# A spectral mixer with a GEGLU FFN: FFN weight groups 3 and 4 loaded early into the buffer of the last down weights, nine half-blocks instead of eight, and one operand read from PSUM

## The chip, the cores and the metric

The kernel runs on one core of one Trainium2 chip. The metric is the device time of one execution in microseconds (us). A core has five engines that run side by side, each with its own instruction queue: TensorE (PE in the profile, with its weight loads as PEld), VectorE (DVE), ScalarE (ACT), GpSimd (POOL) and SyncE (SP). In this kernel SP only issues DMA transfers, in the order of its queue.

## The reference, cut to what matters

```python
def _A_ref(x, w_r, w_i):                       # x: 1 x 2048 x 576, bf16
    X = jnp.fft.rfft2(x.astype(jnp.float32), axes=(-2, -1))
    X = X * (w_r + 1j * w_i)
    return jnp.fft.irfft2(X, s=(S, D), axes=(-2, -1)).astype(jnp.bfloat16)

def _B_ref(x, w_gate, w_up, w_down):           # w_gate, w_up: 576 x 4608; w_down: 4608 x 576
    return (_gelu(x @ w_gate) * (x @ w_up)) @ w_down

h  = x + _A_ref(_layernorm(x), A_w_r, A_w_i)
h2 = h + _B_ref(_layernorm(h), B_w_gate, B_w_up, B_w_down)   # the output
```

## The kernel before, in words

Everything stays on the chip in bf16 and is written out by hand: the program fixes the order of the instructions on each engine (a manual schedule), and the tile pools only decide which buffer a tile gets, so what an instruction waits for is its data, its buffer, and its turn on its engine.

**Spectral part (up to about 68 us).** The 2048 rows are 16 slabs `h` of 128. The two-dimensional FFT is done as products with sine and cosine tables on TensorE. For each of eight pairs of row frequencies (`order` = 1, 2, ..., 7, 0, called channels here) these steps run, staggered over the iterations `i` of one loop:

- `f2` (L478) makes two column transforms in PSUM; `f2_out` (L489) copies each to SBUF as `pq`, on ScalarE.
- `f3(k, 0)` and `f3(k, 1)` (L495, L496) make the row step, each into one PSUM tile `gh_ps`; L514 copies them on ScalarE to SBUF as `g` and `hs`.
- `sums_of(k)` (L523, L524) makes `g - hs` and `g + hs` on VectorE into `xab`.
- `wmul` (L543, L548, L549, L562, L530) multiplies `xab` with the filter on VectorE and leaves the result in `Zt`. The last of these operations for one channel, L530, is held back until the next channel's products are done.
- `i3` (L592) loads `Zt` as weights and transforms back, two iterations after `f3`.
- `inv_cols` (L643) and `add_rows` (L766) finish the inverse transform and `h_sb` becomes `h`.

All PSUM tiles of the kernel share one pool of four tiles (`two`): an engine that still reads one holds up the later matmul that gets its place.

**FFN (from about 68 us).** The 16 slabs go in four chunks of 512 rows. In each chunk the 36 feature blocks `f` of 128 go through `gate` (L894): 18 matmuls give gate and up products in one PSUM tile, ScalarE applies the GELU (L902) and VectorE multiplies (L903) into `P_sb`. Three blocks are one weight group, loaded by `load_gu` (L144) as two DMAs, gate and up, of 432 KB each, in a pool of three buffers. When the three blocks of a group are issued, the group is popped and the group three further on is loaded into its buffer. After the 36 blocks of a chunk the down product runs (L937), with the down weights `w_down` in three buffers of 12 blocks each: `wd_a`, `wd_0` and `wd_1` (the trace calls the last two `wd`).

The start of chunk 0 is special. Its slabs 2 and 3 are not ready when TensorE is, so the first `NH` = 8 blocks are done as **half-blocks**: first on the 256 columns of slabs 0 and 1, later, when blocks 0 to 7 come round in the main loop, on the other 256 columns. In between, slabs 2 and 3 are normalised (`norm2`, L791) and turned by a transposing DMA (`flip`, L803) into `Bt`. The list `after` names what is put between the first half-blocks; the dictionary `todo` puts the remaining work of the spectral part (`fold`, `add_both`, `stats2`, `norm2`, `flip`) and the pieces of the third down-weight buffer (`load_wd2`, L738) behind certain blocks of the main loop.

SP's queue around the change, in order: weight groups 0 to 2 (L144, from 37.69 us on), `wd_a` (L695), the second down-weight buffer (`load_wd(1)`, L728, issued at 59.35 us, when the last reader of the memory that it takes over is done), the flips of slabs 2 and 3 (L803), then group 3 when group 0 is popped, group 4, and so on.

Of the kernel before, what the change touches and what calls it, by code (L numbers as in the profile page):

```python
# [12 lines left out]
BF16 = mybir.dt.bfloat16  # L13
# [7 lines left out]
P = 128  # L21
S = 2048
H = 16
D = 576
# [6 lines left out]
NR = D // 64  # L31
# [3 lines left out]
FQ = 3  # L35
# [6 lines left out]
def kernel_body(  # L42
# [11 lines left out]
    nc = tc.nc  # L54
# [7 lines left out]
    wgpool = ctx.enter_context(tc.tile_pool(name="wgu", bufs=3))  # L62
# [3 lines left out]
    def two(name):  # L66
        return psum.tile([P, 2, 512], FP32, name=name, tag="two", bufs=4)
# [69 lines left out]
            dst, h_sb[:, h, :], m[:, h, 0:1], r[:, h : h + 1], op0=ALU.subtract, op1=ALU.mult  # L137
        )

    def load_gu(g):  # L140
        gc = slice(g % (NFT // FQ) * FQ * P, (g % (NFT // FQ) + 1) * FQ * P)
        t = wgpool.tile([P, NR, FQ * P], BF16, name="wgu", tag="wgu")
        for c, w in ((0, B_w_gate), (1, B_w_up)):
            nc.sync.dma_start(t[64 * c : 64 * c + 64, :, :], w[:, gc].rearrange("(r k) c -> k r c", k=64))  # L144
        return t

    spec = tc.tile_pool(name="spec", bufs=1)
# [8 lines left out]
    wd_view = B_w_down.rearrange("(ft p) d -> p ft d", p=P)  # L156
    NWA = 12
    wd_a = keep.tile([P, NWA, D], BF16, name="wd_a")
# [303 lines left out]
    gk, hk = {}, {}  # L462
    zt = {}
    order = [1, 2, 3, 4, 5, 6, 7, 0]
# [29 lines left out]
    def comb(dst, k1, t0, a, t1, b):  # L494
        T.matmul(dst, lhsT=TF[:, ts[k1], t0, :], rhs=a, start=True, stop=False)  # L495
        T.matmul(dst, lhsT=TF[:, ts[k1], t1, :], rhs=b, start=False, stop=True)  # L496

    def f3(k, half):
        ps = two("gh_ps")
        if k == 0:  # L500
            p0, p8 = pq[0], pq[8]
            t0, t1 = (NS, C) if half else (C, SN)
            for b, kk, p in ((0, 0, p0), (1, 8, p8)):
                comb(ps[:, b, 0:J], kk, t0, p[:, 0, 0:J], t1, p[:, 1, 0:J])
            if half == 0:
                xab[k] = wk.tile([P, 2, 2, JP], BF16, name="xab", tag="xab", bufs=2)
            A.copy(xab[k][:, half, :, 0:J], ps[:, :, 0:J])
            return
        p, q = pq[k], pq[k + 8]
        gh = wk.tile([P, 2, JP], BF16, name="hs" if half else "g", tag="hs" if half else "g", bufs=2)  # L510
        r = half
        comb(ps[:, r, 0:J], k, C, p[:, r, 0:J], SN, q[:, r, 0:J])
        comb(ps[:, 1 - r, 0:J], k, C, q[:, r, 0:J], NS, p[:, r, 0:J])
        A.copy(gh[:, :, 0:J], ps[:, :, 0:J])  # L514
        if half == 0:
            gk[k] = gh
            return
        hk[k] = gh
# [151 lines left out]
    n = len(order)  # L670
    for i in range(n + 1):
# [12 lines left out]
        if 1 <= i <= n:  # L684
            f3(order[i - 1], 0)
            f3(order[i - 1], 1)
            if i == 1:
                f2_out(order[1])
                sums_of(order[0])
            else:  # L690
                if i == 2:
                    cosine(rest)
                    turn_tf(rest)
                    pre = [load_gu(g) for g in range(3)]
                    nc.sync.dma_start(wd_a[:], wd_view[:, 0:NWA, :])  # L695
                wmul(order[i - 2], i - 1, order[i - 1])
# [24 lines left out]
    fp = ctx.enter_context(tc.tile_pool(name="ffn", bufs=1))  # L721
    NP0 = 22
    P_sb = [fp.tile([P, NP0, 4 * P], BF16, name="P_sb")]
    cwb = fp.tile([P, 5, 2, JP], FP32, name="cwb", tag="P1")[:]
    wd = [wd_a] + [fp.tile([P, NWA, D], BF16, name=f"wd_{i}") for i in range(2)]

    def load_wd(i):
        nc.sync.dma_start(wd[i][:], wd_view[:, i * NWA : (i + 1) * NWA, :])  # L728

    def p_sb(f):  # L730
        if f >= NP0 and len(P_sb) == 1:
            P_sb.append(fp.tile([P, NFT - NP0, 4 * P], BF16, name="P_sb", tag="P1"))
        return P_sb[f // NP0][:, f % NP0, :]

    load_wd(1)

    def load_wd2(s):
        nc.sync.dma_start(wd[2][:, s], wd_view[:, 2 * NWA : 3 * NWA][:, s])  # L738


    ln2 = {}
    both = {}
# [128 lines left out]
    todo = {}  # L871
# [8 lines left out]
        todo.setdefault(b + 1, []).append((flip, h))  # L880

    for i in range(0, NWA, 2):
        todo.setdefault(10 + 3 * i // 2, []).append((load_wd2, slice(i, i + 2)))
    blk = 0
    groups = pre
    NG = NFT // FQ

    def gate(tcnk, f, w, i, lo, hi):
        n = hi - lo
        gu = two("gu")  # L890
        for r in range(NR):
            for c in range(2):
                rows = slice(64 * c, 64 * c + 64)
                T.matmul(  # L894
                    gu[:, c, 0:n],
                    lhsT=w[rows, r, i * P : (i + 1) * P],
                    rhs=hl[tcnk % 2][rows, r, lo:hi],
                    start=(r == 0),
                    stop=(r == NR - 1),
                )  # L900
        g_sb = roll.tile([P, D], FP32, name="g_sb", tag="g_sb", bufs=3)[:, 0:n]
        A.activation(g_sb, gu[:, 0, 0:n], ACT.Gelu_apprx_tanh)  # L902
        V.tensor_tensor(p_sb(f)[:, lo:hi], g_sb, gu[:, 1, 0:n], ALU.mult)  # L903

    NH = 8
    after = {
        0: [(sum_squares, 3), (norm2, 2), (flip, 2)],
        1: [(head_rstd, 3)],
        2: [(norm2, 3), (flip, 3)],
    }  # L910
    for f in range(NH):
        gate(0, f, groups[f // FQ], f % FQ, 0, 2 * P)
# [4 lines left out]
    for tcnk in range(4):  # L917
        for gi in range(NG):
            for i in range(FQ):
                f = gi * FQ + i  # L920
                gate(tcnk, f, groups[0], i, 2 * P if tcnk == 0 and f < NH else 0, 4 * P)
                for fn, h in todo.pop(blk, ()):
                    fn(h)
                blk += 1
            groups.pop(0)
            n = tcnk * NG + gi + 3
            if n < 4 * NG:
                groups.append(load_gu(n))
        for st in range(4):
            h = tcnk * 4 + st  # L930
            if h < H - 1:
                accs = [two("acc") for _ in range(2)]
                for f in range(NFT):
                    for c in range(2):
                        for i in range(2):
                            rows = slice(64 * i, 64 * i + 64)
                            T.matmul(  # L937
                                accs[i][:, c, 0:DH],
                                lhsT=p_sb(f)[rows, st * P : (st + 1) * P],
                                rhs=wd[f // NWA][rows, f % NWA, c * DH : (c + 1) * DH],  # L940
                                start=(f == 0),
                                stop=(f == NFT - 1),
                            )
                part = roll.tile([P, D], FP32, name="part", tag="g_sb", bufs=3)[:].rearrange("p (b n) -> p b n", b=2)
                A.copy(part, accs[0][:, :, 0:DH])  # L945
                V.tensor_tensor(part, part, accs[1][:, :, 0:DH], ALU.add)  # L946
                hv = h_sb[:, h, :].rearrange("p (b n) -> p b n", b=2)
                V.tensor_tensor(hv, hv, part, ALU.add)  # L948
                if tcnk == 3:
                    nc.sync.dma_start(out_view[:, h, :], h_sb[:, h, :])  # L950
                continue
            for c in range(2):
                cc = slice(c * DH, (c + 1) * DH)
                acc = two("acc")
                for f in range(NFT):
                    T.matmul(  # L956
                        acc[:, 0, 0:DH],
                        lhsT=p_sb(f)[:, st * P : (st + 1) * P],
                        rhs=wd[f // NWA][:, f % NWA, cc],
                        start=(f == 0),  # L960
                        stop=(f == NFT - 1),
                    )
                V.tensor_tensor(h_sb[:, h, cc], h_sb[:, h, cc], acc[:, 0, 0:DH], ALU.add)
                nc.sync.dma_start(out_view[:, h, cc], h_sb[:, h, cc])
        if tcnk < 3:
            nc.sync.dma_start(
                out_view[:, tcnk * 4 : (tcnk + 1) * 4, :],
                h_sb[:, tcnk * 4 : (tcnk + 1) * 4, :],
            )


@with_exitstack
def kernel(
    ctx: ExitStack,
    tc: tile.TileContext,
    A_x: bass.AP,
    A_w_r: bass.AP,
    A_w_i: bass.AP,
    B_x: bass.AP,
    B_w_gate: bass.AP,  # L980
    B_w_up: bass.AP,
    B_w_down: bass.AP,
    out: bass.AP,
):
    kernel_body(tc, A_x, A_w_r, A_w_i, B_x, B_w_gate, B_w_up, B_w_down, out)
# [30 lines left out]
```

## Time and profile before

| | |
|---|---|
| time, median of 3 runs | 500.18 us (499.68 to 500.25) |
| the profiled execution, its own time | 499.93 us |
| its span in the trace | 498.1 us |
| granted TensorE clock over the span | 0.999 of full speed |
| busy in the span | PE 489.0, PEld 320.1, DVE 223.2, ACT 162.0, POOL 29.3 us |
| DMA traffic | 62.33 MB |

The span is the time between the first and the last recorded work; the 1.8 us beside it belong to the start and the end of the execution. Busy time of an engine is the sum of its instructions' times, with overlaps counted once. Matmuls are pipelined: one has a recorded time of several times the distance to the next one, so a wait looks shorter in the idle column than what it costs.

In a row of the timeline the columns are: start (us), length (us), engine, line, operation, output <- input, shape, xcount, and in brackets the idle time of the engine before it with what ended it. SPq rows are DMA issues in SP's queue. A row of the windows gives, for a stretch of time, the busy time and number of instructions of each engine, then the granted clock, the busy share of the DMA engines, and GB/s.

### The profile page before, as it was taken

The numbers are of one execution on the slowest core, as the hardware profiler recorded it, in microseconds if no ns is written. First come the engines' busy times: TensorE is split into PE (matmuls) and PEld (weight loads), VectorE is DVE, ScalarE is ACT, GpSimd is POOL, SyncE is SP. The second block draws the span as 40 slices with busy tenths as digits, with TensorE's granted clock in tenths as the row PEclk, the third lists the DMA queues.
The fourth block names the chain that finished last, engine by engine and source line by source line (L and its number), as shares of the span: only waits on it lengthen the run. The fifth ranks groups of instructions, "written<-read, shape, count | busy, mean of one in ns | idle before, by whom it ended". The sixth has DMA issues, their size and how long they took to land.

```text
span 498.1 us, 12611 instructions
## 1 busy us (share of the span) xinstructions
PE 489.0 (98%) x5642; PEld 320.1 (64%) x5644; DVE 223.2 (45%) x442; ACT 162.0 (33%) x287; POOL 29.3 (6%) x78
## 2 busy tenths in 40 slices
PE   7999999999999999999999999999999999999997
PEld 3567788444479964444499944444799644445995
DVE  8989786788641234433311245333211333333111
ACT  8989983232210013223200132332110223233000
POOL 8500010101100000000000000000000000000000
PEclk9999999999999999999999999999999999999999
DMA  8729845999990019998830079987700288880000
GB/s 280 222 60 194 217 140 102 204 208 213 192 193 15 2 50 185 205 176 154 158 76 3 3 159 191 193 160 153 145 3 3 71 157 158 158 150 2 14 13 25
DMA packets 89549, 62.33 MB, mean 125 GB/s; under 512 B 23190, under 2 KB 88086, under 8 KB 89494
## 3 DMA queue, kind: packets, MB, share of 16 engines
q1 hardware_dynamic: 89206, 60.34, 61.3%
q0 software_dynamic: 288, 1.18, 0.8%
q8 instruction: 44, 0.72, 0.6%
q14 instruction: 11, 0.09, 0.1%
HBM read 52.65 MB, written 2.36 MB: 110 GB/s over the span
## 4 chain that ended last, share of the span: by engine, by line
PE 90%; DMA 2%; ACT 0%; SPq 0%; issue 0%; DVE 0%
PE gu L894 54%; PE acc L937 27%; PE cs_ps L643 2%; PE acc L956 2%; PE eo_ps L592 2%; DMA wgu<-in_B_w_up_dram 1%; PE pq_ps L478 1%; PE y_ps L766 1%; DMA Bt<-hrow 1%; PE gh_ps L496 0%; PE gh_ps L495 0%; PE eo_ps L616 0%; PE pt L835 0%; ACT hs L514 0%; SPq L144 0%; ACT pq L489 0%
## 5 line engine op out<-in xcount | busy, mean ns | idle before, releaser
L894 PE MATMUL gu<-Bt,wgu 64*128 64x512 bf16 (+1 forms) x2736 | 284.5, 365 | 0.7 <-DMA wgu<-in_B_w_up_dram 0.5
L894 PEld LDWEIGHTS <-wgu 64*128 64x128 bf16 x2736 | 135.0, 94 | 146.1 <-DMA wgu<-in_B_w_up_dram 1.4
L903 DVE TENSOR_TENSOR P_sb<-g_sb,gu 128x512 bf16<-128x512 f32 (+1 forms) x152 | 99.6, 657 | 144.7 <-ACT g_sb L902 144.7
L902 ACT ACTIVATE g_sb<-gu 128x512 f32<-128x512 f32 (+1 forms) x152 | 87.3, 575 | 195.0 <-PE gu L894 194.7
L937 PEld LDWEIGHTS <-P_sb 64*128 64x128 bf16 x2160 | 132.7, 94 | 0.6
L937 PE MATMUL acc<-wd,P_sb 64*128 64x288 bf16 x1440 | 93.8, 283 | 0.0
L946 DVE TENSOR_TENSOR part<-part,acc 128x576 f32<-128x576 f32 x15 | 11.3, 754 | 111.3 <-ACT part L945 111.3
L937 PE MATMUL acc<-wd_a,P_sb 64*128 64x288 bf16 x720 | 49.7, 283 | 0.0
L945 ACT COPY part<-acc 128x576 f32<-128x576 f32 x15 | 9.6, 639 | 122.4 <-PE acc L937 122.4
L285 PE MATMUL f2t<-h_sb,ident 128*128 128x512 bf16 x26 | 9.1, 510 | 3.6 <-DMA h_sb<-in_A_x_dram 3.6
L478 PE MATMUL pq_ps<-DT,Bt 128*128 128x290 bf16 x64 | 12.2, 286 | 0.2 <-DVE Bt L327 0.2
L791 DVE TENSOR_SCALAR hrow<-h_sb,mv,rstd 128x1152 bf16<-128x1152 bf16 x14 | 12.1, 867 | 0.6 <-POOL rstd L829 0.6
L948 DVE TENSOR_TENSOR h_sb<-h_sb,part 128x576 bf16<-128x576 bf16 x15 | 11.4, 758 | 0.5
L133 POOL TENSOR_TENSOR rstd<-rstd,mhalf 128x1 f32<-128x1 f32 (+1 forms) x16 | 11.2, 701 | 1.3
L643 PE MATMUL cs_ps<-DQ,EO 58*128 58x290 bf16 x144 | 11.0, 283 | 0.0
L478 PEld LDWEIGHTS <-Bt 128*128 128x128 bf16 x96 | 9.3, 97 | 2.6
L132 POOL TENSOR_SCALAR rstd<-mv 128x1 f32<-128x1 f32 (+1 forms) x16 | 3.9, 246 | 101.1 <-DVE mv L118 100.8
L297 PE MATMUL f2t<-F,xn 128*128 128x256 bf16 x64 | 9.2, 275 | 0.6 <-DVE xn L136 0.6
L489 ACT CAST pq<-pq_ps 128x580 bf16<-128x580 f32 x15 | 9.6, 668 | 0.0
L123 ACT ACTIVATE junk<-h_sb 128x576 bf16<-128x576 bf16 x14 | 9.4, 676 | 0.4 <-DMA h_sb<-in_A_x_dram 0.4
L643 PEld LDWEIGHTS <-EO 58*128 58x128 bf16 x160 | 8.3, 94 | 2.0 <-issue 0.4
L117 DVE BATCH_NORM_STATS2 st<-h_sb 128x6 f32<-128x288 bf16 x21 | 9.3, 442 | 0.0
(135 smaller groups left out, 265.7 us busy)
## 6 DMA issues: line engine op xcount, KB each, us to landing
wgu<-in_B_w_gate_dram SPq DMA_DIRECT2D x48, 432.0 KB
wgu<-in_B_w_up_dram SPq DMA_DIRECT2D x48, 432.0 KB
wd_a<-in_B_w_down_dram SPq DMA_DIRECT2D x1, 1728.0 KB
wd<-in_B_w_down_dram SPq DMA_DIRECT2D x1, 1728.0 KB
wd<-in_B_w_down_dram SPq DMA_DIRECT2D x6, 288.0 KB
out_dram<-h_sb SPq DMA_DIRECT2D x3, 576.0 KB
h_sb<-in_A_x_dram SPq DMA_DIRECT2D x4, 288.0 KB
h_sb<-in_A_x_dram SPq DMA_DIRECT2D x2, 576.0 KB
```

What stands on the lines that cost most here:

```text
L133: G.tensor_tensor(dst[:, sl], dst[:, sl], mhalf[:, sl], ALU.pow)
L478: T.matmul(ps[:, par, 0:JP], lhsT=Bt[:, t, col], rhs=DT[:, t // 2, par] if t < 4 else DF[:, par], start=(t == par), stop=(t == 4),)
L592: T.matmul(pv[:, n], lhsT=z[:, a, w].rearrange("p b j -> p (b j)"), rhs=TI[:, ts[k], 1 - a : 3 - a, :], start=(a == 0), stop=(a == 1),)
L643: T.matmul(ps[:, e, 0:JP], lhsT=EO[x][rows, w, 2 * g : 2 * g + 2].rearrange("p h e k l -> p (h e k l)"), rhs=DQ[rows, w] if w or e else DT ...
L791: V.tensor_scalar(hrow[:], h_sb[:, h, :].rearrange("p (r k) -> p r k", k=64).unsqueeze(2).to_broadcast([P, NR, 2, 64]), mv2[:, h, 0:1], rs ...
L894: T.matmul(gu[:, c, 0:n], lhsT=w[rows, r, i * P : (i + 1) * P], rhs=hl[tcnk % 2][rows, r, lo:hi], start=(r == 0), stop=(r == NR - 1),)
L902: A.activation(g_sb, gu[:, 0, 0:n], ACT.Gelu_apprx_tanh)
L903: V.tensor_tensor(p_sb(f)[:, lo:hi], g_sb, gu[:, 1, 0:n], ALU.mult)
L937: T.matmul(accs[i][:, c, 0:DH], lhsT=p_sb(f)[rows, st * P : (st + 1) * P], rhs=wd[f // NWA][rows, f % NWA, c * DH : (c + 1) * DH], start=( ...
L946: V.tensor_tensor(part, part, accs[1][:, :, 0:DH], ALU.add)
L948: V.tensor_tensor(hv, hv, part, ALU.add)
L956: T.matmul(acc[:, 0, 0:DH], lhsT=p_sb(f)[:, st * P : (st + 1) * P], rhs=wd[f // NWA][:, f % NWA, cc], start=(f == 0), stop=(f == NFT - 1),)
```

## The change

It has three parts.

1. The buffer of the third 12 down-weight blocks (tag `wd_2`) is first used as a tile `early` of two weight groups, which has the same size. `load_wd(1)` goes from its place before the FFN to the list `after`, behind the flip of slab 3; in its old place groups 3 and 4 are loaded into `early` (four DMAs). Popping groups 0, 1 and 2 now loads groups 5, 6 and 7; popping 3 and 4 loads nothing; from group 5 on each pop loads the group three further on. The pieces of the third down-weight buffer, which can only come when group 4 has been used, go from behind blocks 10, 13, ..., 25 to behind blocks 16, 19, ..., 31.
2. `NH` is 9 instead of 8: block 8 is also done as two half-blocks.
3. For the first channel (`order[0]` = 1), `f3(1, 1)` leaves its result in PSUM: the ScalarE copy to `hs` is left out, and `sums_of(1)` reads the second operand of both VectorE operations from the PSUM tile (fp32) instead of SBUF (bf16).

```diff
-    def load_gu(g):
+    def load_gu(g, t=None):
         gc = slice(g % (NFT // FQ) * FQ * P, (g % (NFT // FQ) + 1) * FQ * P)
-        t = wgpool.tile([P, NR, FQ * P], BF16, name="wgu", tag="wgu")
+        if t is None:
+            t = wgpool.tile([P, NR, FQ * P], BF16, name="wgu", tag="wgu")[:]
...
         comb(ps[:, 1 - r, 0:J], k, C, q[:, r, 0:J], NS, p[:, r, 0:J])
+        if k == order[0] and half:
+            hk[k] = ps
+            return
         A.copy(gh[:, :, 0:J], ps[:, :, 0:J])
...
-    wd = [wd_a] + [fp.tile([P, NWA, D], BF16, name=f"wd_{i}") for i in range(2)]
+    wd = [wd_a, fp.tile([P, NWA, D], BF16, name="wd_1")]
...
+    def load_wd2(s):
+        if len(wd) == 2:
+            wd.append(fp.tile([P, NWA, D], BF16, name="wd_2", tag="wd_2"))
+        nc.sync.dma_start(wd[2][:, s], wd_view[:, 2 * NWA : 3 * NWA][:, s])
...
-    load_wd(1)
...
+    early = fp.tile([P, 2, NR, FQ * P], BF16, name="wgu_e", tag="wd_2")
+    pre += [load_gu(3 + i, early[:, i]) for i in range(2)]
...
     for i in range(0, NWA, 2):
-        todo.setdefault(10 + 3 * i // 2, []).append((load_wd2, slice(i, i + 2)))
+        todo.setdefault(16 + 3 * i // 2, []).append((load_wd2, slice(i, i + 2)))
...
-    NH = 8
+    NH = 9
     after = {
         0: [(sum_squares, 3), (norm2, 2), (flip, 2)],
         1: [(head_rstd, 3)],
-        2: [(norm2, 3), (flip, 3)],
+        2: [(norm2, 3), (flip, 3), (load_wd, 1)],
     }
...
             groups.pop(0)
-            n = tcnk * NG + gi + 3
-            if n < 4 * NG:
-                groups.append(load_gu(n))
+            n = tcnk * NG + gi
+            if n not in (3, 4):
+                n += 5 if n < 3 else 3
+                if n < 4 * NG:
+                    groups.append(load_gu(n))
```

More of the change, by code (lines that the diff above doesn't have):

```diff
@@ L138, in normalise @@
         )
-    def load_gu(g):
+    def load_gu(g, t=None):
         gc = slice(g % (NFT // FQ) * FQ * P, (g % (NFT // FQ) + 1) * FQ * P)
-        t = wgpool.tile([P, NR, FQ * P], BF16, name="wgu", tag="wgu")
+        if t is None:
+            t = wgpool.tile([P, NR, FQ * P], BF16, name="wgu", tag="wgu")[:]
         for c, w in ((0, B_w_gate), (1, B_w_up)):
-            nc.sync.dma_start(t[64 * c : 64 * c + 64, :, :], w[:, gc].rearrange("(r k) c -> k r c", k=64))
+            nc.sync.dma_start(t[64 * c : 64 * c + 64], w[:, gc].rearrange("(r k) c -> k r c", k=64))
         return t
@@ L733, in p_sb @@
         return P_sb[f // NP0][:, f % NP0, :]
-    load_wd(1)
-    def load_wd2(s):
-        nc.sync.dma_start(wd[2][:, s], wd_view[:, 2 * NWA : 3 * NWA][:, s])
+    early = fp.tile([P, 2, NR, FQ * P], BF16, name="wgu_e", tag="wd_2")
+    pre += [load_gu(3 + i, early[:, i]) for i in range(2)]
     ln2 = {}
```

## The prediction

> **What bounds the kernel now.** I read the page first, then the waits of TensorE, then the chain that ended last in order of time.
>
> ```profile
> span 498.1 us, 12611 instructions
> ...
> PE 489.0 (98%) x5642; PEld 320.1 (64%) x5644; DVE 223.2 (45%) x442; ACT 162.0 (33%) x287; POOL 29.3 (6%) x78
> ```
> ```profile
> PE gh_ps L496 <- ACT pq L489: 0.5, 2, 0.3
> PE gu L894 <- DMA wgu<-in_B_w_up_dram: 0.5, 1, 0.5
> PE gh_ps L495 <- ACT TF L255: 0.2, 1, 0.2
> PE gu L894 <- DMA Bt<-hrow: 0.2, 1, 0.2
> ```
>
> TensorE sets the time: it is busy for 489.0 of 498.1 us. The change removes no TensorE work, so it can only win back waits. The waits list (total us, times, longest) names three that it aims at: `pq` in the spectral part, the up half of a weight group, and the flip. In the chain, behind 68 us, all is TensorE but for these two transfers, start and length in us:
>
> ```profile
> 74.19 3.45 DMA Bt<-hrow
> ```
> ```profile
> 81.60 7.25 DMA wgu<-in_B_w_up_dram
> ```
>
> The flip of slab 3 lands at 74.19 + 3.45 = 77.64, weight group 3 at 81.60 + 7.25 = 88.85.
>
> **What the two FFN waits really cost.** Idle time understates a wait, since a matmul's recorded time runs past the start of the next. I take the loss from the follower: ScalarE's GELU starts once per block.
>
> ```profile
> 77.58 0.38 ACT L902 ACTIVATE g_sb<-gu 128x256 f32<-128x256 f32 x1 [0.60 <-PE gu L894]
> 78.97 0.39 ACT L902 ACTIVATE g_sb<-gu 128x256 f32<-128x256 f32 x1 [1.00 <-PE gu L894]
> ...
> 85.35 0.38 ACT L902 ACTIVATE g_sb<-gu 128x256 f32<-128x256 f32 x1 [0.60 <-PE gu L894]
> 86.33 0.38 ACT L902 ACTIVATE g_sb<-gu 128x256 f32<-128x256 f32 x1 [0.60 <-PE gu L894]
> 88.28 0.60 ACT L902 ACTIVATE g_sb<-gu 128x512 f32<-128x512 f32 x1 [1.56 <-PE gu L894]
> 91.05 0.60 ACT L902 ACTIVATE g_sb<-gu 128x512 f32<-128x512 f32 x1 [2.17 <-PE gu L894]
> ```
>
> An undisturbed half-block takes 86.33 - 85.35 = 0.98 us, an undisturbed full block (block 8) 88.28 - 86.33 = 1.95. Between block 7's first half (77.58) and block 0's second half (78.97) lie 1.39: **0.41 lost** to the flip. Between block 8 (88.28) and block 9 (91.05) lie 2.77: **0.82 lost** to group 3.
>
> **Part 1, groups 3 and 4 early.** What moves is SP's queue.
>
> ```profile
> 59.35 0.37 SPq L728 DMA_DIRECT2D wd<-in_B_w_down_dram  x1
> 72.00 4.28 SPq L803 DMA_TRANSPOSE Bt<-hrow  x2
> 80.93 0.63 SPq L144 DMA_DIRECT2D wgu<-in_B_w_gate_dram  x1
> ```
> ```profile
> 41.50:52.00 10.50, 10.50 (x91) 8.39 (x88) 10.50 (x25) 10.22 (x19) 0.00 (x0) 1.00 1.13 200
> ```
> ```profile
> 78.00:80.00 2.00, 2.00 (x42) 2.00 (x38) 0.84 (x2) 0.43 (x2) 0.00 (x0) 1.00 0.00 0
> 80.00:82.00 2.00, 2.00 (x42) 2.00 (x38) 1.63 (x5) 0.80 (x3) 0.00 (x0) 1.00 0.00 0
> ```
>
> The four new DMAs take the place of the issue at 59.35, behind the same waits, and 4 x 0.63 = 2.5 us of SP's time. Their 4 x 432 KB = 1.77 MB go at the rate of weight groups, 200 GB/s (the window in which groups 0 to 2 arrive), in 8.8 us: landed by about 70, where block 9 needs them at about 87.7. The 0.82 goes whole. They end some 2 us before the flips at 72.00.
>
> `load_wd(1)` is moved past both flips, which end their issue at 76.28. SP has nothing due from there until group 0 is popped, about 81.5, and the DMA engines stand idle (0 GB/s from 78 to 82), so its issue of 0.37 us delays nobody. Its 1.77 MB, at 200 GB/s if it is no faster than a weight group, are in by about 86.5. They are first read in the down product:
>
> ```profile
> 143.96 35.25 PE acc L937 x574
> ```
>
> What is late next? Group 5 is issued at 81.5 and needed by block 15, at 87.7 + 6 x 1.95 = 99.4 at the earliest; with the rest of `wd_1` ahead of it, its 0.88 MB are in by 91. Groups 6 and 7 have as much time. The pieces of the third down buffer come six blocks later; the last, behind block 31, goes out at about 133 (143.96 less the 1.2 won and five blocks), and its first reader, block 34 of the down product, comes 34 x 4 matmuls of 35.25/574 us behind the chunk's end, at about 151. I take 0 for all of it.
>
> **Part 2, the ninth half-block.**
>
> ```profile
> 77.77 5.09 PE L894 MATMUL gu<-Bt,wgu 64*128 64x256 bf16 x90 [0.23 <-DMA Bt<-hrow]
> ```
> ```profile
> 88.97 1.01 DVE L903 TENSOR_TENSOR P_sb<-g_sb,gu 128x256 bf16<-128x256 f32 x2
> ```
>
> Without the wait the second halves would begin at 77.77 - 0.41 = 77.36; with one more half-block in front, at 78.34. The flip lands at 77.64, 0.7 us earlier: the 0.41 goes. The price is two half-blocks for one full block, 2 x 0.98 - 1.95 = **+0.01**, and one more GELU and product on engines that wait for TensorE. What could be late next is VectorE, which is behind there: its products of blocks 7 and 8 end at 88.97 + 1.01 = 89.98; moved by 0.57 with the second halves, about 90.5. The next matmuls to take their PSUM tiles are those behind block 10, at about 87.7 + 3.9 = 91.6. 1.1 us are left; beyond that each us counts whole.
>
> **Part 3, the sum out of PSUM.**
>
> ```profile
> 28.23 0.64 ACT L514 CAST g<-gh_ps 128x578 bf16<-128x578 f32 x1 [0.74 <-PE gh_ps L496]
> 28.76 0.65 ACT L514 CAST hs<-gh_ps 128x578 bf16<-128x578 f32 x1
> ```
> ```profile
> 29.44 0.47 DVE L523 TENSOR_TENSOR xab<-g,hs 128x578 bf16<-128x578 bf16 x1 [0.79 <-ACT hs L514]
> 29.82 0.46 DVE L524 TENSOR_TENSOR xab<-g,hs 128x578 bf16<-128x578 bf16 x1
> 30.37 0.77 DVE L543 TENSOR_TENSOR m<-xab,WR 128x1156 bf16<-128x1156 bf16 x1
> ```
> ```profile
> 83.65 1.41 DVE L777 TENSOR_TENSOR h_sb<-h_sb,y_ps 128x576 bf16<-128x576 bf16 x2
> ```
> ```profile
> 61.22 0.82 DVE L663 TENSOR_SCALAR cs<-cs_ps 128x580 bf16<-128x580 f32 x1 [1.50 <-PE cs_ps L643]
> ```
>
> L523 now waits for `hs`, which ends at 29.41. After the change it waits for `g`, which ends at 28.87, so it starts at about 28.90, 0.54 earlier. But its second operand is then fp32 in PSUM. The nearest row is L777, the same operation on a bf16 and a PSUM operand of 576: two in 1.41. From 28.90 the pair ends at 30.31. L543 starts 0.09 behind the end of L524 (29.82 + 0.46 = 30.28) now, so 30.40 then: **+0.03**. Bounds: the pair could keep today's 0.84, giving -0.54; by L663, the slowest VectorE read of PSUM that I found, 2 x 0.82 give +0.26. I take the row with the same operation.
>
> [...]
>
> Does the 0.03 reach the end?
>
> ```profile
> 30.40:35.60 5.20, 4.57 (x33) 3.00 (x32) 5.10 (x11) 5.01 (x9) 0.00 (x0) 1.00 0.15 32
> ```
> ```profile
> 35.12 0.45 DVE L530 TENSOR_TENSOR Zt<-zb,za 128x580 bf16<-128x580 bf16 x1
> ```
> ```profile
> 35.64 1.00 PEld L592 LDWEIGHTS <-Zt 128*128 128x128 bf16 x10 [0.36 <-issue]
> ```
> ```profile
> 30.55 0.28 PE L496 MATMUL gh_ps<-pq,TF 128*128 128x289 bf16 x1 [0.26 <-ACT pq L489]
> ```
>
> VectorE is busy for 5.10 of the 5.20 us behind L543, up to L530, which ends at 35.57; `i3` loads that `Zt` as weights and starts at 35.64, after a gap. So this chain passes its shift on. Dropping a ScalarE copy of 0.65 also lets `pq` come earlier, and the wait at 30.55 (and its like in the next channel) shrinks; but TensorE then meets the same 35.64. I take 0 for that, and +0.03 for the part.
>
> **Sum:** -0.82 - 0.41 + 0.01 + 0.03 = **-1.19 us**, on the profiled execution 499.93 -> 498.74. That execution is 0.25 under the median of the runs, 500.18, which I take as the base: 500.18 - 1.19 = **499.0**. I call 0.2% (1.0 us) the bound, about what a measurement of this kernel can tell from no change; the forecast lies just beyond it.
>
> **Rivals.**
>
> *A wait stays (inside the bound).* `wd_1` goes out right behind flip 3 (76.28), which lands only at 77.64; if it shares the DMA engines with the flip, the flip may lose its 0.7 to spare and more, up to the 0.41 again. Or part 3 costs L663's 0.26. Then -1.19 + 0.41 = -0.78, or -1.19 + 0.23 = -0.96: about 499.3. For it: L663 exists. Against it: group 3, issued at 80.93, moved nothing before 82, so a new DMA comes late for that; and L777 is the closer operation.
>
> *ScalarE is the releaser (more gain).* The chain in order of time has this in front of `i3`:
>
> ```profile
> 34.97 0.66 ACT hs L514
> ```
>
> It ends at 35.63. If ScalarE's queue sets that start, one copy less moves it by the 0.4 that TensorE loses at 30.55 (0.26 idle and its overlap): -1.6, 498.6. Against it: `Zt` comes from L530 at 35.57, and VectorE's chain in front has no hole, so at best 0.06 should come of it.
>
> *Early groups block the flips (slower).* The place is the DMA engines at 72.00. Group 3 itself took from 80.93 to 88.85, 7.9 us for 0.88 MB, 112 GB/s. At that rate groups 3 and 4 would land at 59.35 + 15.8 = 75.2; the flips queued behind would land 3.2 late, at 80.8, and the second halves start there, 2.5 after the forecast's 78.34: -1.19 + 2.5 = +1.3, 501.5. It decides from a landing after 72.7 on (below 133 GB/s). Against it: 200 GB/s held over 10.5 us with groups back to back, and those 7.9 us hold the start-up and the first part of group 4.
>
> **Chances and range.** Forecast 0.62, a wait stays 0.22, ScalarE 0.08, flips blocked 0.06, others, half of them slower, 0.02. Since the runs of before spread over 0.57, a sixth of the forecast's share falls within the bound. Faster by over 0.2%: 0.52 + 0.08 = 0.60; within: 0.10 + 0.22 = 0.32; slower by over 0.2%: 0.08, rounded up. The range for 8 in 10 goes from the ScalarE case less half the spread, 498.3, to a kept wait and the dear end of part 3 together (-1.19 + 0.41 + 0.23 = -0.55) plus that half, 499.9.
>
> **What would show it.** Right: no wait of L894 for `wgu` or `Bt` in the profile after; GELU starts 0.98 apart across the turn from first to second halves and 1.95 from block 9 to 10; the pair of sums from 28.9 to 30.3, and `i3`'s first weight load at 35.7. Wrong: a new wait of TensorE near 91.6 (PSUM tiles) or 99 (group 5), flips landing after 78.3, `i3` starting well before 35.6, or the down product waiting for `wd`.

## The result and the profile after

| | before | after |
|---|---|---|
| median | 499.98 us (499.68 to 500.72, 10 runs) | 498.65 us (498.43 to 499.50, 10 runs) |
| profiled execution: span | 498.1 us | 496.9 us |

The ratio is 0.9974, 95% interval 0.9965 to 0.9984: 1.33 us less at the medians, 0.8 to 1.75 by the interval. The forecast was 1.19 less. The two profiled executions took 499.93 and 498.63 us, 1.30 apart. Lines of code that lie behind the edits have moved by 1, 4, 7 or 9: gate is now L901, GELU L909, flip L810, `i3` L596, the sums L527 and L528, the held sum L534, the down product L946.

The page and the waits of TensorE after:

```profile
span 496.9 us, 12651 instructions
...
PE 487.9 (98%) x5662; PEld 357.5 (72%) x5662; DVE 223.9 (45%) x443; ACT 161.7 (33%) x287; POOL 29.2 (6%) x78
```
```profile
PE f2t L286 <- DMA h_sb<-in_A_x_dram: 3.7, 1, 3.7
PE f2t L298 <- DVE xn L136: 0.8, 3, 0.3
PE eo_ps L596 <- ACT hs L518: 0.5, 1, 0.5
```

No FFN matmul is left in the waits: neither `wgu` nor `Bt` is named. (Block 33 still loses 0.10 by the ledger below, less than this list shows.) ScalarE's GELU shows the same, by the start of each block:

```profile
78.48 0.38 ACT L909 ACTIVATE g_sb<-gu 128x256 f32<-128x256 f32 x1 [0.60 <-PE gu L901]
79.46 0.38 ACT L909 ACTIVATE g_sb<-gu 128x256 f32<-128x256 f32 x1 [0.60 <-PE gu L901]
...
87.81 0.38 ACT L909 ACTIVATE g_sb<-gu 128x256 f32<-128x256 f32 x1 [0.60 <-PE gu L901]
89.75 0.60 ACT L909 ACTIVATE g_sb<-gu 128x512 f32<-128x512 f32 x1 [1.56 <-PE gu L901]
91.70 0.60 ACT L909 ACTIVATE g_sb<-gu 128x512 f32<-128x512 f32 x1 [1.34 <-PE gu L901]
```

The first two rows are the last of the nine first halves and the first of the nine second halves: 0.98 apart, nothing lost at the turn. Block 9 (89.75) follows the second half of block 8 (87.81) at 1.94, and block 10 follows at 1.95. Block 9 stands 1.30 earlier than before (91.05); 0.13 of that is the start of the program, as shown below.

SP's queue after, where `wgu_e` is the tile `early`:

```profile
59.28 0.61 SPq L145 DMA_DIRECT2D wgu_e<-in_B_w_gate_dram  x1
...
71.92 4.62 SPq L810 DMA_TRANSPOSE Bt<-hrow  x2
76.60 0.58 SPq L732 DMA_DIRECT2D wd<-in_B_w_down_dram  x1
81.42 0.62 SPq L145 DMA_DIRECT2D wgu<-in_B_w_gate_dram  x1
```

And windows of the same kernel (the last number is GB/s, the one before it the DMA engines' busy share):

```profile
68.00:70.00 2.00, 2.00 (x40) 1.87 (x38) 1.53 (x6) 1.52 (x5) 0.00 (x0) 1.00 0.93 165
70.00:72.00 2.00, 2.00 (x40) 1.88 (x38) 1.69 (x6) 1.55 (x6) 0.55 (x1) 1.00 0.04 11
...
80.00:82.00 2.00, 2.00 (x41) 1.82 (x39) 1.44 (x5) 0.77 (x2) 0.00 (x0) 1.00 1.09 384
```

The early groups are in by about 70 (165 GB/s falls to 11), before the flips are issued at 71.92; `wd_1` fills the stretch behind 78 that was empty before.

Part 3, in the timelines of ScalarE, VectorE and TensorE's weight loads after:

```profile
28.10 0.64 ACT L518 CAST g<-gh_ps 128x578 bf16<-128x578 f32 x1 [0.74 <-PE gh_ps L497]
...
34.48 0.65 ACT L518 CAST hs<-gh_ps 128x578 bf16<-128x578 f32 x1
```
```profile
28.78 0.76 DVE L527 TENSOR_TENSOR xab<-g,gh_ps 128x578 bf16<-128x578 bf16 x1 [0.25 <-ACT g L518]
29.45 0.75 DVE L528 TENSOR_TENSOR xab<-g,gh_ps 128x578 bf16<-128x578 bf16 x1
30.30 0.77 DVE L547 TENSOR_TENSOR m<-xab,WR 128x1156 bf16<-128x1156 bf16 x1
...
35.05 0.46 DVE L534 TENSOR_TENSOR Zt<-zb,za 128x580 bf16<-128x580 bf16 x1
```
```profile
35.58 1.00 PEld L596 LDWEIGHTS <-Zt 128*128 128x128 bf16 x10 [0.79 <-issue]
```

The start of the whole program varies: in the profiled executions of all kernels here the first `g` copy lies between 27.98 and 28.88. So I measure from it: it lies at 28.10 after and at 28.23 before, which is 0.13 of the 1.30 between the two executions and no part of the change. From the copy to the products (L547) it takes 2.20, before 2.14; to the first weight load of `i3` 7.48, before 7.41. From the copy to the first down product (L946, at 142.41; before L937, at 143.68) it takes 114.31, before 115.45: **1.14 less**. That is what these two traces show of the change; how it stands to the 1.33 of the medians is dealt with below.

**A ledger of losses.** From the GELU starts of any kernel the loss at a place is the distance to the GELU before, less 0.98 for a half-block or 1.94 to 1.95 for a full one. (Blocks that have the `y_ps` matmuls in front take 0.48 to 0.50 more in every kernel; these aren't counted.) In us, one profiled execution each, as are the two start columns; the last column is the ratio of all runs:

| kernel | flip | block 9 | block 33 | sum | `g` to `i3` | `g` to down product | ratio to before, 95% |
|---|---|---|---|---|---|---|---|
| before | 0.41 | 0.82 | 0.08 | 1.31 | 7.41 | 115.45 | |
| after | 0 | 0 | 0.10 | 0.10 | 7.48 | 114.31 | 0.9974 (0.9965 to 0.9984) |
| part 3 alone | 0.78 | 0.82 | 0 | 1.60 | 7.47 | 115.78 | 1.0004 (0.9995 to 1.0013) |
| parts 1 and 2 | 0 | 0 | 0.15 | 0.15 | 7.42 | 114.28 | 0.9969 (0.9957 to 0.9980) |
| part 1 | 0.91 | 0 | 0 | 0.91 | 7.42 | 115.21 | 0.9980 (0.9971 to 0.9989) |
| part 2 | 0 | 1.11 | 1.57 | 2.68 | 7.42 | 116.85 | 1.0034 (1.0018 to 1.0049) |
| part 2, late pieces | 0 | 1.21 | 0.64 | 1.85 | 7.42 | 116.00 | 1.0007 (0.9997 to 1.0016) |
| before, late pieces | 0.85 | 0.54 | 0 | 1.39 | 7.42 | 115.51 | 0.9995 (0.9986 to 1.0004) |
| after, `wd_1` first | 2.52 | 0 | 0 | 2.52 | 7.47 | 116.89 | 1.0025 (1.0014 to 1.0035) |
| after, release early | 0 | 0 | 0 | 0 | 6.72 | 114.41 | 0.9971 (0.9959 to 0.9982) |
| after, two from PSUM | 0 | 0 | 0 | 0 | 8.11 | 114.95 | 0.9981 (0.9972 to 0.9990) |

### The profile page after: what moved, and what is told of

Same layout as the page of the kernel before. It is cut to its first block, busy times and chain, and to the rows that moved or that the text cites. A ratio compares the mean times of both kernels' runs of the same rounds, so it can differ in the third digit from the quotient of the medians.

```text
span 496.9 us, 12651 instructions
## 1 busy us (share of the span) xinstructions
PE 487.9 (98%) x5662; PEld 357.5 (72%) x5662; DVE 223.9 (45%) x443; ACT 161.7 (33%) x287; POOL 29.2 (6%) x78
## 4 chain that ended last, share of the span: by engine, by line
PE 92%; ACT 0%; issue 0%; DVE 0%
PE gu L901 56%; PE acc L946 27%; PE cs_ps L647 2%; PE acc L965 2%; PE eo_ps L596 2%; PE pq_ps L479 1%; PE y_ps L773 1%; PE gh_ps L497 0%; PE gh_ps L496 0%; PE eo_ps L620 0%; PE pt L842 0%; ACT g L518 0%; ACT pq L490 0%; ACT hs L518 0%; DVE h_sb L972 0%
## 5 line engine op out<-in xcount | busy, mean ns | idle before, releaser
L901 PE MATMUL gu<-Bt,wgu 64*128 64x512 bf16 (+1 forms) x2646 | 271.9, 363 | 0.0
L901 PEld LDWEIGHTS <-wgu 64*128 64x128 bf16 x2646 | 162.1, 94 | 106.2 <-DMA wgu<-in_B_w_up_dram 0.3
L909 ACT ACTIVATE g_sb<-gu 128x512 f32<-128x512 f32 (+1 forms) x153 | 87.5, 572 | 193.6 <-PE gu L901 193.3
L946 PEld LDWEIGHTS <-P_sb 64*128 64x128 bf16 x2160 | 132.7, 94 | 0.5
L946 PE MATMUL acc<-wd,P_sb 64*128 64x288 bf16 x1440 | 93.5, 283 | 0.0
L946 PE MATMUL acc<-wd_a,P_sb 64*128 64x288 bf16 x720 | 49.4, 283 | 0.0
L901 PE MATMUL gu<-Bt,wgu_e 64*128 64x512 bf16 x108 | 12.2, 376 | 0.0
L901 PEld LDWEIGHTS <-wgu_e 64*128 64x128 bf16 x108 | 10.0, 94 | 1.4
```

The lines of the kernel that those rows point to most:

```text
L901: T.matmul(gu[:, c, 0:n], lhsT=w[rows, r, i * P : (i + 1) * P], rhs=hl[tcnk % 2][rows, r, lo:hi], start=(r == 0), stop=(r == NR - 1),)
L946: T.matmul(accs[i][:, c, 0:DH], lhsT=p_sb(f)[rows, st * P : (st + 1) * P], rhs=wd[f // NWA][rows, f % NWA, c * DH : (c + 1) * DH], start=( ...
```

## The experiments

**Part 3 alone.** The kernel before with this edit; `sums_of` then reads the PSUM tile without an edit of its own:

```diff
+        if k == order[0] and half:
+            hk[k] = ps
+            return
         A.copy(gh[:, :, 0:J], ps[:, :, 0:J])
```

> Part 3 alone (the first channel's sums take hs from PSUM; groups 3 and 4 and the half-blocks as before). Theory 'two FFN waits': the sums start 0.54 us earlier and last 0.57 longer, VectorE's chain behind them has no hole, so the time changes by +0.03 to +0.07 us, not measurable; in the trace L543 starts 2.14 to 2.21 us and the first weight load of i3 7.41 to 7.48 us behind the start of the first channel's g copy (before: 30.37 - 28.23 = 2.14 and 35.64 - 28.23 = 7.41); both FFN waits stay, 0.41 and 0.82. Rival 'ScalarE's relief': one copy less frees 0.4 us, i3's first weight load comes 7.0 us behind the g copy and the time falls by 0.4 us.

Measured: 500.21 against 500.04 us, ratio 1.0004 (0.9995 to 1.0013). `i3` starts 0.06 later behind the `g` copy. The theory holds: no gain, and any loss is too small for this measurement. That ScalarE's dropped copy brings 0.4 is outside the interval.

**Parts 1 and 2 without part 3.** Against the changed kernel:

```diff
-        if k == order[0] and half:
-            hk[k] = ps
-            return
```

> Parts 1 and 2 without part 3 (the hs copy of the first channel is back on ScalarE). Theory 'two FFN waits': -1.22 us against the kernel before, as large as the whole change or 0.03 to 0.07 larger; no wait of TensorE for wgu or Bt in the trace. Rival 'ScalarE's relief': about 0.4 us less of a gain than the whole change, -0.8 to -0.9 us.

Measured: 498.41 against 500.04, ratio 0.9969. The whole gain is there without part 3. It is the quickest median of the study, 0.24 under the whole change, but the intervals overlap; the two traces differ by 0.03 at the down product, so a lead over the whole change is not shown.

**Part 1 alone.** Against the kernel with parts 1 and 2:

```diff
-    NH = 9
+    NH = 8
```

> Part 1 alone: groups 3 and 4 early, eight half-blocks, hs copied. Theory 'two FFN waits': -0.82 us; the wait for the flip stays, GELU starts 1.39 us apart at the turn from first to second halves, none for group 3 (1.95 between blocks 8 and 9). Rival 'the moved transfers delay the flip': the flip lands later than 77.7 us and its loss grows beyond 0.41, so the gain is smaller than 0.82.

Measured: 499.06 against 500.04, ratio 0.9980: 0.98 less. The wait for the group is gone, the one for the flip stays. Its waits and its GELU at the turn:

```profile
PE gu L898 <- DMA Bt<-hrow: 0.7, 1, 0.7
```
```profile
77.55 0.38 ACT L906 ACTIVATE g_sb<-gu 128x256 f32<-128x256 f32 x1 [0.60 <-PE gu L898]
79.44 0.38 ACT L906 ACTIVATE g_sb<-gu 128x256 f32<-128x256 f32 x1 [1.50 <-PE gu L898]
```

1.89 - 0.98 = 0.91 is lost here, twice what the profile of before showed for the same wait. The rival put such a loss down to the moved transfers. But the kernels "part 3 alone" and "before, late pieces", whose transfers up to there are those of before, lose 0.78 and 0.85 to the flip, so these traces don't show that the moved transfers do it. In this execution the gain up to the down product was only 115.45 - 115.21 = 0.24; the median of 11 runs says 0.98. That other executions lose less to the flip is likely, but the trace of one can't show it. Parts 1 and 2 together, measured beside the same runs of before, have a median of 498.41: on top of part 1, the ninth half-block is worth 0.65.

**Part 2 alone**, the kernel before with

```diff
-    NH = 8
+    NH = 9
```

> Part 2 alone: nine half-blocks, groups 3 and 4 loaded when groups 0 and 1 are popped, as before. Theory 'the parts are coupled': the ninth half-block removes the flip's 0.41 but moves the second halves, and with them the pop of group 0 and the issue of group 3, by 0.57 us; group 3 lands 7.9 us behind its issue whatever TensorE does, so block 9 starts 0.57 us LATER than before: +0.57 us, slower, with a wait for wgu of about 1.8 us in place of 0.82. Rival 'the parts add up': -0.40 us.

Measured: 501.40 against 500.04, ratio 1.0034 (1.0018 to 1.0049): **slower by 1.36**. The flip's wait is gone, and two longer ones stand in its place. Waits, GELU and the transfers on the chain of this kernel:

```profile
PE gu L894 <- DMA wgu<-in_B_w_up_dram: 2.2, 2, 1.4
```
```profile
88.54 0.38 ACT L902 ACTIVATE g_sb<-gu 128x256 f32<-128x256 f32 x1 [0.60 <-PE gu L894]
91.60 0.60 ACT L902 ACTIVATE g_sb<-gu 128x512 f32<-128x512 f32 x1 [2.67 <-PE gu L894]
...
138.24 0.60 ACT L902 ACTIVATE g_sb<-gu 128x512 f32<-128x512 f32 x1 [1.34 <-PE gu L894]
141.76 0.60 ACT L902 ACTIVATE g_sb<-gu 128x512 f32<-128x512 f32 x1 [2.92 <-PE gu L894]
```
```profile
82.83 6.58 DMA wgu<-in_B_w_up_dram
129.87 9.69 DMA wgu<-in_B_w_up_dram
```

Block 9 loses 1.11 and block 33, the first of group 11, 1.57. With the 0.41, 0.82 and 0.08 of before that is 2.68 - 1.31 = +1.37 in these two executions, against 1.36 at the medians. The rival, that the flip's 0.41 is won by itself, is refuted.

But the theory's mechanism is not what the trace shows. It expected the whole loss at block 9: a wait of 1.8 and a start 0.57 later than before. The up half of group 3 does go out 0.59 later, 53.96 behind the `g` copy (at 28.87 here) instead of 53.37. It then takes 6.58 instead of 7.25, and lands at 60.54 behind the copy, before at 60.62. Block 9 starts with that landing, so it starts about where it did: its 1.11 is a little less than the 0.41 + 0.82 of before. What the flip no longer costs is spent in waiting for group 3.

The loss is at block 33, and that was not foreseen. These are rows of before for the same group 11, its up half in SP's queue and the GELU of block 33:

```profile
129.42 1.18 SPq L144 DMA_DIRECT2D wgu<-in_B_w_up_dram  x1
```
```profile
139.71 0.60 ACT L902 ACTIVATE g_sb<-gu 128x512 f32<-128x512 f32 x1 [1.43 <-PE gu L894]
```

In part 2 alone block 33's GELU starts 2.20 behind the landing (129.87 + 9.69 = 139.56). Counted back from 139.71, the up half took at most 8.1 in before, an estimate from these rows; here it took 9.69. It went out no later (101.00 behind the `g` copy, before 101.20), and the bytes of the stretch are the same (204 GB/s between 100 and 140 us, before 203). So the transfer itself was slower; why it is so with the ninth half-block stays open.

**The same kernel once more**, one execution:

> Nine half-blocks without the early groups, a second look at its trace. If its two waits for wgu (1.1 us lost at block 9, 1.6 at block 33 in the first look) belong to the kernel, both come again; if the one at block 33 was a chance of one execution, it is gone and the time is about that of the kernel before.

Measured: 501.75 us, one run. Both waits are there again, 1.10 at block 9 and 1.34 at block 33: no accident of one execution.

**Part 2 with the pieces of the third down buffer late.**

```diff
-        todo.setdefault(10 + 3 * i // 2, []).append((load_wd2, slice(i, i + 2)))
+        todo.setdefault(16 + 3 * i // 2, []).append((load_wd2, slice(i, i + 2)))
...
-    NH = 8
+    NH = 9
```

> Part 2 alone (nine half-blocks), with the six pieces of the third down-weight buffer moved from behind blocks 10 to 25 to behind blocks 16 to 31, as the whole change has them. Theory: the second wait of part 2 alone (1.57 us lost at block 33) is a matter of bytes: the last piece, 0.29 MB, goes out just ahead of group 11, and at 200 GB/s it is worth 1.5 us; with the pieces late the last one goes out behind group 11. That wait goes, the one at block 9 (1.11 lost) stays, the flip's loss is gone: 1.36 - 1.5 = -0.1, between -0.5 and +0.2 of the kernel before. Rival: the wait comes from SP's queue, held by the transposing DMA of 5.8 us ahead of group 11 whatever the pieces do: it stays, +1.4.

Measured: 500.22 against 500.16, ratio 1.0007 (0.9997 to 1.0016). GELU at block 33 and the transfer:

```profile
137.69 0.60 ACT L902 ACTIVATE g_sb<-gu 128x512 f32<-128x512 f32 x1 [1.35 <-PE gu L894]
140.27 0.60 ACT L902 ACTIVATE g_sb<-gu 128x512 f32<-128x512 f32 x1 [1.98 <-PE gu L894]
```
```profile
127.78 10.30 DMA wgu<-in_B_w_up_dram
```

By the clock group 11 lands at 138.08 instead of 139.56, but this execution started 0.64 earlier (`g` copy at 28.23, in part 2 alone at 28.87). From the copy it lands 0.84 earlier, and 0.64 of the wait stays. That is less than the 1.5 that one piece was to be worth, and that the wait would go whole was a miss. The rival, that it would stay whole, is refuted too. The two causes are not separated by this run: a piece still goes out just ahead of group 11 (the fourth of the six; two now follow behind it), and the transposing DMA in front of it holds SP's queue for 4.28 us, where it held it for 5.77.

**Only the pieces late**, the first of those two edits alone.

> The kernel before, with only the six pieces of the third down-weight buffer moved from behind blocks 10 to 25 to behind blocks 16 to 31. Theory: it has no wait there to win but 0.07 us at block 33, so the time is that of the kernel before, between -0.2 and 0. Rival: the late pieces themselves are part of the whole change's gain, by 0.3 or more (the 1.33 measured against the 1.19 forecast would then be theirs). Other side: the last piece, out at about 133, is late for the down product, and TensorE waits there for wd: slower.

Measured: 499.98 against 500.16, ratio 0.9995 (0.9986 to 1.0004): no difference that can be told. This part of part 1 doesn't carry the whole gain. The rival's 0.3 lies inside the interval, so the times don't refute it, but from the `g` copy to the down product the trace has 115.51, before 115.45: nothing won there. No wait for `wd` came of it. Its GELU at the turn and at block 9 show something else:

```profile
77.34 0.38 ACT L902 ACTIVATE g_sb<-gu 128x256 f32<-128x256 f32 x1 [0.60 <-PE gu L894]
79.17 0.38 ACT L902 ACTIVATE g_sb<-gu 128x256 f32<-128x256 f32 x1 [1.44 <-PE gu L894]
...
88.47 0.60 ACT L902 ACTIVATE g_sb<-gu 128x512 f32<-128x512 f32 x1 [1.56 <-PE gu L894]
90.96 0.60 ACT L902 ACTIVATE g_sb<-gu 128x512 f32<-128x512 f32 x1 [1.89 <-PE gu L894]
```

0.85 and 0.54 are lost, where before lost 0.41 and 0.82, with the same code up to there. What the two have to do with each other is taken up below.

**The whole change, with `wd_1` back in front of the FFN** (behind groups 3 and 4).

```diff
+    load_wd(1)
...
-        2: [(norm2, 3), (flip, 3), (load_wd, 1)],
+        2: [(norm2, 3), (flip, 3)],
```

> The whole change, but the second down-weight buffer (load_wd(1)) is issued right behind the early groups 3 and 4, ahead of the flips, instead of behind them. Theory 'the flips need a free DMA': groups 3 and 4 are in by about 70, the 1.77 MB of wd_1 behind them take some 4.6 us more, to about 74.5, and the flips issued at 72 and 74 queue behind it; they land 1 to 2.5 us later than 77.6, past TensorE's 78.35, so 0.3 to 1.6 us of the gain go: -1.0 to +0.3 us against the kernel before, with a wait for Bt. Rival 'the place of wd_1 does not matter' (flips share the DMA engines and keep their time): -1.3 us as the whole change, no wait for Bt.

Measured: 500.98 against 500.20, ratio 1.0025 (1.0014 to 1.0035): slower than the kernel before, more than I expected. Windows, the transfer on the chain, and GELU at the turn:

```profile
72.00:74.00 2.00, 2.00 (x41) 1.98 (x36) 1.69 (x7) 1.47 (x3) 0.55 (x1) 1.00 1.09 357
...
78.00:80.00 2.00, 0.31 (x5) 0.03 (x1) 0.62 (x2) 0.38 (x1) 0.00 (x0) 1.00 1.21 68
```
```profile
74.50 6.01 DMA Bt<-hrow
```
```profile
78.34 0.38 ACT L910 ACTIVATE g_sb<-gu 128x256 f32<-128x256 f32 x1 [0.60 <-PE gu L902]
81.84 0.38 ACT L910 ACTIVATE g_sb<-gu 128x256 f32<-128x256 f32 x1 [3.11 <-PE gu L902]
```

`wd_1` is still coming in at 357 GB/s when the flips go out; the flip of slab 3 lands at 80.51, 2.87 later than before, and 3.50 - 0.98 = 2.52 are lost. So the new place of `wd_1` is worth 2.5 us in this execution, more than the whole gain. By the medians it is about 2.1 (0.78 slower than before instead of 1.33 quicker).

**The held sum released early**, for the first channel:

```diff
-            if k in order[5:7]:
+            if k == order[0] or k in order[5:7]:
```

> The whole change, and the held last VectorE operation of the first channel (L534 in the kernel after) is done right behind that channel's first Zt operation instead of behind the next channel's products. It comes 1.35 us earlier, so i3's first weight load comes when TensorE is ready, 6.85 us behind the g copy's start instead of 7.48 (35.58 - 28.10). Theory 'VectorE's whole chain bounds the spectral part': TensorE then meets the same chain at the next channels, nothing of the 0.6 reaches the FFN; -1.2 to -1.3 us as the whole change. Rival 'from there TensorE bounds': the 0.6 us stay, -1.9 us.

Measured: 498.77 against 500.20, ratio 0.9971, as the whole change. The weight loads of `i3`, first and second channel:

```profile
34.94 1.09 PEld L596 LDWEIGHTS <-Zt 128*128 128x128 bf16 x10
39.44 1.00 PEld L596 LDWEIGHTS <-Zt 128*128 128x128 bf16 x10 [0.97 <-issue]
```

The first starts 6.72 behind the `g` copy instead of 7.48, so it is VectorE's `Zt` that releases it. The second starts 11.22 behind it instead of 39.19 - 28.10 = 11.09: the 0.76 is given back one channel later, with 0.1 on top. VectorE's chain over the channels sets the pace, and the order within it buys nothing.

**The second channel's sums from PSUM as well.**

```diff
-        if k == order[0] and half:
+        if k in order[0:2] and half:
```

> The whole change, with the second channel's sums out of PSUM as well (part 3 done twice). VectorE is busy without a hole there, so nothing starts earlier, and its two operations take 0.58 us longer (0.67 instead of 0.37 from start to start, twice). Theory 'VectorE's chain is the path': +0.58 against the whole change, -0.7 us against the kernel before; i3 of the second channel's Zt 0.58 later. Rival 'ScalarE's relief': one ScalarE copy less again, the time falls by up to 0.4 more, -1.7 us.

Measured: 499.30 against 500.20, ratio 0.9981 (0.9972 to 0.9990). VectorE in the second channel, and `i3`:

```profile
32.69 0.75 DVE L527 TENSOR_TENSOR xab<-g,gh_ps 128x578 bf16<-128x578 bf16 x1
33.36 0.75 DVE L528 TENSOR_TENSOR xab<-g,gh_ps 128x578 bf16<-128x578 bf16 x1
```
```profile
36.32 1.00 PEld L596 LDWEIGHTS <-Zt 128*128 128x128 bf16 x10 [1.97 <-issue]
```

In this channel VectorE was not waiting for ScalarE, so nothing is won by leaving out the copy, and each sum takes 0.67 from start to start instead of 0.37: 2 x 0.30 = 0.60. `i3` comes 0.63 later, the down product 114.95 - 114.31 = 0.64 later. In these two traces, what VectorE loses in this stretch reaches the FFN whole. The medians, 0.90 less than before against 1.33, fit this, but the two intervals overlap.

## Why the prediction was right

**The -0.82 for group 3: right.** With groups 3 and 4 early, no kernel here lost anything at block 9; without, all lost 0.54 to 1.21. The landing by about 70 at 200 GB/s was right too: from 62 to 68 the windows of after have 195 to 229 GB/s.

**The -0.41 for the flip: right in kind, small in size.** The same wait cost 0.78, 0.85 and 0.91 in three other executions with eight half-blocks. In the chains of these four, the flip of slab 3 is 3.45, 3.82, 3.89 and 3.95 long, so all of the difference lies in the transfer; why it varies isn't shown. The ninth half-block took the wait away in every kernel whose flips weren't held up. I took one execution's loss as the kernel's, and it was the smallest of the four.

That the number came so near is in part luck. The FFN losses of before, of part 3 alone and of the late pieces add up to 1.31, 1.60 and 1.39. Less the 0.10 that stays at block 33 and the 0.07 of part 3, the gain would be 1.14 to 1.43 from one execution to another. The 1.14 of the traces and the 1.33 of the medians both lie in that, and so does the forecast.

**Two terms that I added are not independent.** Each was costed against the kernel before, and the sum came out since both parts are there. These are the up halves of group 3, start and length, in part 3 alone, in the late pieces and in part 2 with late pieces:

```profile
81.82 7.23 DMA wgu<-in_B_w_up_dram
```
```profile
81.80 6.97 DMA wgu<-in_B_w_up_dram
```
```profile
82.17 6.68 DMA wgu<-in_B_w_up_dram
```

They land at 89.05, 88.77 and 88.85, in before at 88.85 and in part 2 alone at 89.41. In all five, the GELU of block 9 starts 2.19 to 2.20 later. So as long as group 3 comes late, its landing sets where block 9 starts. What the flip or the ninth half-block costs ahead of it only shifts when group 3 goes out, and the landing follows that only in part: from the `g` copy, these up halves go out 0.43 to 0.59 later than in before, and land between 0.08 earlier and 0.42 later. The 0.41 + 0.82 of before become 0 + 1.21 in part 2 with late pieces, with the same landing. In these runs, taking away the flip's wait was worth something only on top of part 1 (0.65 by the medians). Part 2 alone is not -0.41 but +1.36. In the prediction I had not asked what the ninth half-block would do if the early groups weren't there.

**The +0.03 of part 3: right, to a few hundredths.** Predicted for the products was 0.03 later; measured from the `g` copy 0.06, at `i3` 0.07, at the end nothing that the measurement can tell. The pair took 28.78 to 30.20, against 28.90 to 30.31. For a sum from PSUM the rows show 0.67 from start to start and 0.75 to 0.76 in length, against 0.37 and 0.46 from SBUF in the second channel of the kernel after.

**The rivals.** *ScalarE is the releaser* is refuted three times: part 3 alone wins nothing, an early release moves `i3`, two sums from PSUM delay it. The waits after still name `hs` for `i3`, though by its row it ended at 35.13 and `Zt` at 35.51, just ahead of 35.58. *A wait stays* didn't come about: `wd_1`, issued at 76.60 behind the flips, let them land before they were needed. *Early groups block the flips* didn't either, as the groups were in by 70; but its mechanism is real. It took `wd_1` ahead of the flips to bring it on, at 2.52 us. That this equals the rival's price of 2.5 is chance: the rival had other bytes in front, at 112 GB/s, and my expectation for this run was that 0.3 to 1.6 of the gain would go.

**Costed at nothing.** VectorE's products of block 8 end at 90.22 and the next matmul on that pool starts at 91.40: 1.2 to spare, forecast 1.1. Group 5 and `wd_1` were waited for nowhere. What I had not seen is a gain in reserve: from 100 to 140 us the DMA engines have room again, since groups 3 and 4, 1.77 MB, no longer come in behind 81 us, and `wd_1` takes the time that was idle between 78 and 82. The windows of before and after (a busy share above 1 means that recorded times of packets overlap):

```profile
100.00:140.00 40.00, 40.00 (x384) 18.92 (x382) 30.14 (x61) 11.63 (x20) 5.54 (x14) 1.00 1.16 203
```
```profile
100.00:140.00 40.00, 40.00 (x385) 33.43 (x382) 29.53 (x59) 11.90 (x20) 4.73 (x12) 1.00 0.98 182
```

In before, block 33 was on the edge (0.08 lost), and part 2 alone went over it (1.57). With part 1 as well, the same ninth half-block loses 0.10 to 0.15 there. That the room is the reason is inferred.

## What to carry to other kernels

Two waits on one stream of loads are not two terms: where the landing of a later load sets the pace, taking away an earlier wait wins nothing until that load comes early as well (the ninth half-block: +1.36 us alone, -0.65 on top of part 1). A loss read from one execution can be half of what the next one shows (the flip: 0.41 and 0.78 to 0.91). A large load that nobody needs soon belongs behind the small transfers that somebody waits for, even if the queue has time for it earlier (`wd_1` ahead of the flips: 2.52 lost). And before leaving out a copy, see whether its engine is the one that is waited for: by start and end of the rows, not by the name in the waits.

## What the runs showed of the hardware

A transposing DMA held SP's queue for 1.3 to 5.8 us, and how busy the DMA engines are doesn't alone explain it. This is the second of the four flips of slabs 4 to 7, before and after:

```profile
110.67 3.31 SPq L803 DMA_TRANSPOSE Bt<-hrow  x1
```
```profile
109.37 1.33 SPq L810 DMA_TRANSPOSE Bt<-hrow  x1
```

While they were held, the busy share of the DMA engines was 1.14 in both. The first of the four took 2.14 before and 1.32 after, the last 5.40 and 3.65. What was queued behind such a DMA went out when it was done, the next weight group too: in before the last one ended at 122.62 + 5.40 = 128.02, the next piece of the down weights went out at 128.07 and group 11 at 128.75. What sets the time wasn't tried.

The down weights came in at 384 GB/s in the window from 80 to 82 us at a busy share of 1.09, weight groups at about 200 GB/s at 1.13. I had put `wd_1` at the rate of a weight group; which property of the two loads makes the difference wasn't tried.

The busy time of PEld is no measure of the load on TensorE: 320.1 us before, 357.5 after, for 18 weight loads more in 5662 and less time. The kernel with the early release has 416.5 us for the same 5662.

In two of the ten runs of part 2 alone (503.75 and 504.21 us) and in three of the ten with `wd_1` first (502.43 to 502.88 us), the granted TensorE clock was 0.996 to 0.997; in every other run whose clock is on record it was 0.999 or 1.000. These two kernels have the longest waits of FFN matmuls for a transfer in their profiles (1.4 and 2.3 us by the waits). No run with the lower clock was profiled, so what brought it down is not shown. Without these five runs the two medians would be 0.15 and 0.03 lower.
